# A three-instruction exponential on VectorE with one term made by GpSimd, a shorter rsqrt chain and earlier head preparation in a normalized attention kernel

## The chip, the cores and the metric

The kernel runs on one core of a Trainium2 chip. The metric is device time in microseconds (us). Before the change two runs took 858.82 and 860.21 us, median 859.52. One further execution was profiled; it took 857.78 us, and its span from first to last instruction is 855.5 us.

Names of engines: PE is TensorE (its weight loads are listed as PEld), DVE is VectorE, ACT is ScalarE, POOL is GpSimd, SP is SyncE, whose queue (SPq) issues all DMAs here.

## What is computed

Attention with normalized queries and keys for 32 heads of 2048 positions and 20 channels, in bf16. There is no mask, and no maximum is subtracted, since the logits are bounded by t, which is near 1.

```python
qn = q / (sqrt((q*q).sum(-1)) + eps)
kn = k / (sqrt((k*k).sum(-1)) + eps)
logits = einsum('bhqd,bhkd->bhqk', qn, kn) * t[h]
out = einsum('bhqk,bhkd->bhqd', softmax(logits), v)
```

The costly part is the exponential of 32 x 2048 x 2048 logits.

## The kernel before

**Tiling.** The keys of a head are cut into R = 16 chunks of 128 keys. For one chunk the 2048 queries form four units of 512 (index g). A chunk of logits therefore is a tile of 128 keys by 2048 queries. Most chunks get their exponential on ACT; some get it on DVE. `DVE_TILES` (line 177) says how many chunks of each head go to DVE: 3, 3, 3, 4 and again, so 13 of every 64, 104 of 512 in all. The other 408 chunks are 1632 units for ACT.

**ACT path** (`add_wave`, lines 379 to 404). Three units make a wave: PE writes three products of 128x512 into one half of `psA` (six banks of PSUM, two halves), and ACT takes the exponential of all 1536 columns in one instruction into `p_ring`. There are 544 waves. Where two of the units belong to different halves of the row groups, PE works them side by side with 64 rows each.

**DVE path** (`add_dtile`, lines 417 to 459). It builds the exponential from the bits of an fp16 number. For each of the four units of a chunk, PE writes the logits into `psD`, the only bank for this path, and DVE makes `xt = int16(x * 1024 * log2(e) + offset)`, called t1 here (line 430). Read as fp16, `xt` is a power of two with a linear mantissa. Four further instructions on the whole 128x2048 chunk correct the mantissa: `rr` (an xor, line 435), `mm` (the mantissa as a number in [1, 2), line 437), `tt = xt * mm` (line 440) and `uu = tt * mm` (line 443). PE then adds three products to the output: `xt` with 8 v, `rr` with 2 v, and `uu` with v. The scaled copies `v8` and `v2` are made by POOL once per head (lines 278 to 281).

**Output.** All products of probabilities and values of a head add up in `psO`, one bank. `pv_mm` (line 346) issues four matmuls, one per column group. When a head is complete, DVE transposes `psO` (line 360), takes a reciprocal and scales (`add_fin`), and SP stores the result.

**Preparation of a head** (`add_prep`, line 259). SP loads q, k and v; DVE squares, sums, and makes a reciprocal square root by the integer start value and two Newton steps (lines 290 to 308), in ten small instructions plus the scaling by t; DVE writes the normalized rows `qkn` (line 310). SP then issues a DMA transpose to `qkT` (line 315), four copies to `qz` (line 321) and six rotated copies to `kR` (line 327). The matmuls of the head wait for all of these. `qkT`, `qz` and `kR` have three buffers, so the transpose of head h also waits for the last logits product of head h - 3.

**The order of work.** Every piece is a task with an engine, an assumed duration, dependencies and a due value, in units of heads. `schedule` (line 51) plays the tasks through once with the assumed durations: a free engine takes the ready task with the smallest due value. That gives each engine a fixed order, in which the engine then waits by semaphores. A head's preparation is due at h - 1.6; t1 and the products that feed it have a bonus, so they go ahead of everything else on DVE; the four chunk-wide instructions are due about when ACT reaches that part of the head. `plan_waits` drops waits that others imply.

Of the kernel before, what the change touches and what calls it, by code (L numbers as in the profile page):

```python
# [9 lines left out]
BF16 = mybir.dt.bfloat16  # L10
FP16 = mybir.dt.float16
F32 = mybir.dt.float32
# [4 lines left out]

KEXP = 12.9958  # L20
LOG2E = math.log2(math.e)
X_MUL = 1024.0 * LOG2E
X_ADD = 1024.0 * (15.0 - math.log2(KEXP))


class Task:
# [10 lines left out]
class Program:  # L37
# [8 lines left out]
    def add(self, eng, name, fn, dur, deps=(), pri=0.0, lat=0.0, dma=None):  # L46
        t = Task(eng, name, fn, dur, deps, pri, lat, dma)
        self.tasks.append(t)
        return t
# [54 lines left out]
    def plan_waits(self, sem_of):  # L104
        pos = {}
        for e, ts in self.order.items():
            for i, t in enumerate(ts):
                pos[t.seq] = i
        for t in self.tasks:
            for d in t.deps:  # L110
                if not d.dma and (d.eng != t.eng or d.eng == "DVE"):
                    d.inc = True
        dma_cnt = {}
        for e, ts in self.order.items():
            c = 0
            for t in ts:
                if t.dma:
                    dma_cnt[t.dma] = dma_cnt.get(t.dma, 0) + 16
                    t.cnt = dma_cnt[t.dma]
                elif t.inc:  # L120
                    c += 1
                    t.cnt = c
        allt = sorted(self.tasks, key=lambda t: (t.start, t.seq))
        known = {e: {} for e in self.order}
        snap = {}
        waits = {}
        for t in allt:
            kn = known[t.eng]
            need = {}
            for d in t.deps:  # L130
                if not d.dma and d.eng == t.eng and d.eng != "DVE":
                    continue
                key = d.dma if d.dma else d.eng
                if need.get(key, (0, None))[0] < d.cnt:
                    need[key] = (d.cnt, d)
            ws = []
            for key, (c, d) in sorted(need.items(), key=lambda kv: -kv[1][1].end):
                if kn.get(key, 0) >= c:
                    continue
                ws.append((key, c))  # L140
                kn[key] = c
                for k2, c2 in snap[d.seq].items():
                    if kn.get(k2, 0) < c2:
                        kn[k2] = c2
            waits[t.seq] = ws
            snap[t.seq] = dict(kn)
        self.waits = waits
# [12 lines left out]
def bass_standalone__qk_norm__prompt_kernel(  # L160
# [13 lines left out]
    NB = 4  # L174
    NT = 3
    NX = 3
    DVE_TILES = [4 if h % 4 == 3 else 3 for h in range(H)]
    PE_GROUP = 0.27
    VD = 4

    with ExitStack() as es:
        sbuf = lambda name, shape, dt: es.enter_context(nc.sbuf_tensor(name, shape, dt))
# [3 lines left out]
        act_scr = sbuf("act_scr", [128, 32], F32)  # L186
        qk_sb = [sbuf(f"qk_sb{i}", [128, 2 * R, D], BF16) for i in range(NB)]
        vaug = [sbuf(f"vaug{i}", [128, R, 32], BF16) for i in range(NB)]
        v2 = [sbuf(f"v2{i}", [128, VD, 32], BF16) for i in range(NB)]
        v8 = [sbuf(f"v8{i}", [128, VD, 32], BF16) for i in range(NB)]  # L190
        sq = sbuf("sq", [128, 2 * R, D], F32)
        rs = {x: sbuf(f"rs_{x}", [128, 2 * R], F32) for x in ("sum", "u", "a", "b", "c", "y", "r")}
        qkn = [sbuf(f"qkn{i}", [128, 2 * R, 32], BF16) for i in range(2)]
        qkT = [sbuf(f"qkT{i}", [128, 8 * 128], BF16) for i in range(NT)]
        qz = [sbuf(f"qz{i}", [128, NG, 512], BF16) for i in range(NT)]
        kR = [sbuf(f"kR{i}", [128, 3, 512], BF16) for i in range(NT)]
        p_ring = sbuf("p_ring", [128, NP * 512], BF16)
        xt = [sbuf(f"xt{i}", [128, 2048], I16) for i in range(NX)]
        rr = [sbuf(f"rr{i}", [128, 2048], I16) for i in range(NX)]
        mm = [sbuf(f"mm{i}", [128, 2048], I16) for i in range(2)]  # L200
        tt = [sbuf(f"tt{i}", [128, 2048], FP16) for i in range(2)]
        uu = [sbuf(f"uu{i}", [128, 2048], FP16) for i in range(NX)]
        oT = sbuf("oT", [128, R, 32], F32)
        rec = sbuf("rec", [128, R], F32)
        o_stage = [sbuf(f"o_stage{i}", [128, R * D], BF16) for i in range(2)]
# [40 lines left out]
            return h + (i - a0[h]) / nA_head[h]  # L246


        ld_qk, ld_v, norm, trn, rot, vsc = {}, {}, {}, {}, {}, {}
        qk_users = {h: [] for h in range(H)}  # L250
        pv_users = {h: [] for h in range(H)}
        vs_users = {h: [] for h in range(H)}

        def bc(ap2d, n):
            return bass.AP(ap2d.tensor, ap2d.offset, [ap2d.ap[0], [1, n], [0, D]])
# [2 lines left out]

        def add_prep(h):
            b, b2, bt = h % NB, h % 2, h % NT  # L260
            due = h - 1.6
            war = [norm[h - NB]] if h >= NB else []
            lds = []
            for nh in range(4):
# [6 lines left out]
            lds.append(add("SP", f"ldk{h}", lambda eng, tk: eng.dma_start(qk_sb[b][:, R:2 * R, :], src_k),  # L271
                           0.6, war, due - 0.5, lat=2.5, dma=f"k{b}"))
            src_v = v[0, h].rearrange("(p r) d -> p r d", p=128)
            warv = (pv_users[h - NB] + vs_users[h - NB] + [vsc[h - NB]]) if h >= NB else z_v[b]
            ld_v[h] = add("SP", f"ldv{h}", lambda eng, tk: eng.dma_start(vaug[b][:, :, 0:D], src_v),
                          0.6, warv, due - 0.4, lat=3.0, dma=f"v{b}")

            def vscale(eng, tk):
                eng.tensor_scalar(v2[b][:, :, :], vaug[b][:, R - VD:R, :], 2.0, None, ALU.mult)  # L279
                return eng.tensor_scalar(v8[b][:, :, :], vaug[b][:, R - VD:R, :], 8.0, None, ALU.mult)  # L280
            vsc[h] = add("POOL", f"vsc{h}", vscale, 0.8, [ld_v[h]] + z_v[b], due)

            def dv(name, fn, dur, deps):
                return add("DVE", name + str(h), fn, dur, deps, due)
# [2 lines left out]
                    0.75, lds + prep_deps)]  # L287
            c.append(dv("sum", lambda eng, tk: eng.tensor_reduce(rs["sum"][:, :], sq[:, :, :], AXIS_X, ALU.add),
                        0.75, [c[-1]]))
            c.append(dv("rs", lambda eng, tk: eng.tensor_single_scalar(  # L290
                rs["u"][:, :].bitcast(I32), rs["sum"][:, :].bitcast(I32), 1, ALU.logical_shift_right), 0.12, [c[-1]]))
            c.append(dv("rs", lambda eng, tk: eng.tensor_scalar(
                rs["u"][:, :].bitcast(I32), rs["u"][:, :].bitcast(I32), 1597463007, -1, ALU.subtract, ALU.mult),
                0.12, [c[-1]]))
            cur = rs["u"]
            for it in range(2):
                c.append(dv("rs", lambda eng, tk, cur=cur: eng.tensor_tensor(
                    rs["a"][:, :], cur[:, :], cur[:, :], ALU.mult), 0.12, [c[-1]]))
                c.append(dv("rs", lambda eng, tk: eng.tensor_tensor(
                    rs["b"][:, :], rs["a"][:, :], rs["sum"][:, :], ALU.mult), 0.12, [c[-1]]))  # L300
                c.append(dv("rs", lambda eng, tk: eng.tensor_scalar(
                    rs["c"][:, :], rs["b"][:, :], -0.5, 1.5, ALU.mult, ALU.add), 0.12, [c[-1]]))
                tgt = rs["r"] if it == 1 else rs["y"]
                c.append(dv("rs", lambda eng, tk, cur=cur, tgt=tgt: eng.tensor_tensor(
                    tgt[:, :], cur[:, :], rs["c"][:, :], ALU.mult), 0.12, [c[-1]]))
                cur = rs["y"]
            c.append(dv("rs", lambda eng, tk: eng.tensor_scalar(
                rs["r"][:, 0:R], rs["r"][:, 0:R], t_f32[:, h:h + 1], None, ALU.mult), 0.12, [c[-1], tcp]))
            war = [trn[h - 2]] if h >= 2 else [z_qkn[b2]]
# [69 lines left out]
        def add_wave(w):  # L379
# [13 lines left out]
            deps = [act.get(w - 2)]  # L393
            for h in hs:
                deps += [trn[h]] + rot[h]
            qk = add("PE", f"qkA{w}", f_qk, 0.22 * (len(us) - 1), deps, due_a(us[0]) - 100)
            for h in hs:
                qk_users[h].append(qk)
            p0 = us[0] % NP
# [17 lines left out]
        def add_dtile(j):  # L417
# [7 lines left out]
            for ii in range(NG):  # L425
# [6 lines left out]
                    [qk] + old.get("x", []), due - 5)  # L432
                t1_prev[0] = t1
                t1s.append(t1)
            tr_ = add("DVE", f"r{j}", lambda eng, tk: eng.tensor_single_scalar(  # L435
                rr[s][:, :], xt[s][:, :], 0x3FF, ALU.bitwise_xor), 0.60, t1s + old.get("r", []), due)
            tm = add("DVE", f"m{j}", lambda eng, tk: eng.tensor_scalar(  # L437
                mm[s2][:, :], xt[s][:, :], 0x3FF, 0x3C00, ALU.bitwise_and, ALU.bitwise_or), 0.60,
                t1s + old2.get("m", []), due)
            tT = add("DVE", f"T{j}", lambda eng, tk: eng.tensor_tensor(  # L440
                tt[s2][:, :], xt[s][:, :].bitcast(FP16), mm[s2][:, :].bitcast(FP16), ALU.mult), 1.13,
                [tm] + old2.get("t", []), due)
            tU = add("DVE", f"U{j}", lambda eng, tk: eng.tensor_tensor(  # L443
                uu[s][:, :], tt[s2][:, :], mm[s2][:, :].bitcast(FP16), ALU.mult), 1.13,
                [tT] + old.get("u", []), due)
            b = h % NB
            rv = r - (R - VD)
            base = [vsc[h]] + ([trO[h - 1]] if h else [])

            def pv(nm, tile, wt, deps):  # L450
                p = add("PE", f"pv{nm}{j}", lambda eng, tk: pv_mm(
                    eng, h, wt, lambda g: tile[:, 512 * g:512 * g + 512].bitcast(FP16)), PE_GROUP, deps + base, due + 0.2)
                pv_users[h].append(p)
                return p
            pS = pv("S", xt[s], v8[b][:, rv, :], t1s)
            pR = pv("R", rr[s], v2[b][:, rv, :], [tr_])
            pU = pv("U", uu[s], vaug[b][:, r, :], [tU])
            vs_users[h] += [pS, pR, pU]
            x_users[j] = {"x": [tr_, tm, tT, pS], "r": [pR], "m": [tT, tU], "t": [tU], "u": [pU]}

        d0 = [sum(DVE_TILES[:h]) for h in range(H + 1)]
        nw = ng = 0
# [75 lines left out]
```

## Time and profile before

| | busy, us | share of the span | instructions |
|---|---|---|---|
| PE | 706.3 | 83% | 4836 |
| DVE | 783.2 | 92% | 1380 |
| ACT | 749.7 | 88% | 546 |
| POOL | 52.9 | 6% | 79 |

| | us |
|---|---|
| span of the profiled execution | 855.5 |
| device time of the profiled execution | 857.78 |
| median of two runs | 859.52 |

The time outside the span is thus about 2.3 us, and the profiled execution is 1.7 us under the median. The first matmul starts at 29.4 us and the first exponential of ACT at 30.6 us: until then the first heads are loaded, normalized, transposed and rotated. The mean granted clock of PE is 0.960.

A group of instructions is read as line, engine, operation, what is written and read, count, then busy time and mean duration, then the idle time of the engine just ahead of it and what ended that idle time. Durations in the records of DVE and ACT overlap a little from one instruction to the next, so the sum of the durations on DVE is more than its busy time.

### The profile page before, as it was taken

How to read it: one execution, taken by the hardware profiler on the slowest of the kernel's cores; microseconds unless marked ns; L12 is line 12 of the kernel's file. 1: busy time of each engine (PE TensorE's matmuls, PEld its weight loads, DVE VectorE, ACT ScalarE, POOL GpSimd, SP SyncE). 2: the span in 40 equal slices, each digit the busy share in tenths (PEclk: the TensorE clock that was granted, in tenths of full speed). 3: DMA queues.
4: the chain of work that ended last, by engine and by line, in shares of the span. 5: the costliest groups of instructions: out<-in, count | busy, mean ns of one | idle time of the engine just before them, and what ended most of it. 6: DMA issues, size and time to landing. Idle time of an engine off the chain costs nothing.

```text
span 855.5 us, 12498 instructions
## 1 busy us (share of the span) xinstructions
PE 706.3 (83%) x4836; PEld 201.5 (24%) x4928; DVE 783.2 (92%) x1380; ACT 749.7 (88%) x546; POOL 52.9 (6%) x79
## 2 busy tenths in 40 slices
PE   0598998989887988788986998959988798898887
PEld 0122222222222222122221222212222122222122
DVE  7699998989998999799987999879998899999798
ACT  0599999989999899799986999859998799999797
POOL 3000000001000000000000101000000000000000
PEclk9999999999999999899997999979999899999799
DMA  6441203331213330413314213042121421220200
GB/s 54 89 65 30 49 10 53 53 52 23 47 38 54 53 53 5 67 35 53 47 14 67 54 32 53 8 77 44 31 44 18 80 34 37 45 41 22 66 1 8
DMA packets 198346, 36.49 MB, mean 43 GB/s; under 512 B 173712, under 2 KB 198288, under 8 KB 198288
## 3 DMA queue, kind: packets, MB, share of 16 engines
q1 hardware_dynamic: 198288, 35.70, 25.4%
q8 instruction: 38, 0.62, 0.3%
q14 instruction: 20, 0.16, 0.1%
HBM read 7.87 MB, written 2.62 MB: 12 GB/s over the span
## 4 chain that ended last, share of the span: by engine, by line
DVE 51%; PE 26%; SPq 13%; DMA 4%; issue 3%; ACT 2%
DVE xt L430 19%; PE psA L342 12%; DVE tt L440 9%; PE psO L351 8%; DVE uu L443 8%; PE psD L342 6%; SPq L327 5%; SPq L321 4%; DVE mm L437 3%; SPq L268 3%; DMA kR<-qkT 3%; DVE rr L435 3%; ACT p_ring L402 2%; DVE qkn L310 2%; DVE oT L360 2%
## 5 line engine op out<-in xcount | busy, mean ns | idle before, releaser
L402 ACT ACTIVATE p_ring<-psA 128x1536 bf16<-128x1536 f32 x544 | 748.2, 1463 | 100.4 <-PE psA L342 84.2
L342 PE MATMUL psA<-qz,kR 64*128 64x512 bf16 (+1 forms) x1169 | 316.1, 401 | 61.5 <-DMA kR<-qkT 43.7
L430 DVE TENSOR_SCALAR xt<-psD 128x512 int16<-128x512 f32 x416 | 284.1, 683 | 55.2 <-PE psD L342 50.1
L351 PE MATMUL psO<-p_ring,vaug 128*32 128x512 bf16 x1632 | 165.6, 396 | 8.4 <-issue 5.3
L342 PEld LDWEIGHTS psA<-qz,kR 64*128 64x128 bf16 (+1 forms) x1224 | 85.1, 94 | 267.9 <-issue 163.7
L342 PE MATMUL psD<-qz,kR 128*128 128x512 bf16 x296 | 119.2, 403 | 34.4 <-DVE xt L430 15.7
L342 PE MATMUL psA<-qz,qkT 64*128 64x512 bf16 (+1 forms) x395 | 133.3, 400 | 5.3 <-DMA kR<-qkT 1.8
L443 DVE TENSOR_TENSOR uu<-tt,mm 128x2048 f16<-128x2048 f16 x104 | 126.6, 1217 | 0.0
L440 DVE TENSOR_TENSOR tt<-xt,mm 128x2048 f16<-128x2048 f16 x104 | 126.5, 1216 | 0.1
L435 DVE TENSOR_SCALAR rr<-xt 128x2048 int16<-128x2048 int16 x104 | 71.4, 686 | 0.2
L437 DVE TENSOR_SCALAR mm<-xt 128x2048 int16<-128x2048 int16 x104 | 71.3, 685 | 0.0
L351 PEld LDWEIGHTS psO<-p_ring,vaug 128*32 128x32 bf16 x1632 | 42.0, 93 | 110.7 <-issue 100.9
L279 POOL TENSOR_SCALAR v<-vaug 128x128 bf16<-128x128 bf16 x32 | 21.7, 677 | 701.8 <-DMA vaug<-in_v_dram 701.8
L351 PE MATMUL psO<-uu,vaug 128*32 128x512 f16 x416 | 41.8, 392 | 19.8 <-DVE uu L443 18.7
L342 PEld LDWEIGHTS psD<-qz,kR 128*128 128x128 bf16 x312 | 30.3, 97 | 96.3 <-DVE xt L430 57.7
L342 PEld LDWEIGHTS psA<-qz,qkT 64*128 64x128 bf16 (+1 forms) x408 | 32.6, 94 | 68.6 <-issue 51.7
L351 PE MATMUL psO<-xt,v 128*32 128x512 f16 x416 | 41.4, 388 | 8.1 <-DVE oT L360 5.8
L342 PE MATMUL psD<-qz,qkT 128*128 128x512 bf16 x96 | 38.4, 400 | 6.5 <-DVE xt L430 4.7
L351 PE MATMUL psO<-rr,v 128*32 128x512 f16 x416 | 41.2, 386 | 1.5 <-DVE rr L435 1.1
L286 DVE TENSOR_TENSOR sq<-qk_sb 128x640 f32<-128x640 bf16 x32 | 26.2, 819 | 3.4 <-DMA qk_sb<-in_k_dram 3.2
L280 POOL TENSOR_SCALAR v<-vaug 128x128 bf16<-128x128 bf16 x32 | 27.4, 856 | 2.0
L360 DVE STREAM_TRANSPOSE oT<-psO 128x512 f32<-128x512 f32 x32 | 22.7, 710 | 5.2 <-PE psO L351 4.9
(29 smaller groups left out, 190.9 us busy)
## 6 DMA issues: line engine op xcount, KB each, us to landing
kR<-qkT SPq DMA_DIRECT2D x64, 96.0 KB, 2.1
qz<-qkT SPq DMA_DIRECT2D x128, 32.0 KB, 1.9
kR<-qkT SPq DMA_DIRECT2D x64, 64.0 KB, 2.0
qk_sb<-in_q_dram SPq DMA_DIRECT2D x128, 20.0 KB, 2.5
qk_sb<-in_k_dram SPq DMA_DIRECT2D x32, 80.0 KB, 2.5
vaug<-in_v_dram SPq DMA_DIRECT2D x32, 80.0 KB, 3.2
out_dram<-o_stage SPq DMA_DIRECT2D x32, 80.0 KB, 1.9
kR<-qkT SPq DMA_DIRECT2D x64, 32.0 KB, 1.9
```

The source lines that it names most:

```text
L280: return eng.tensor_scalar(v8[b][:, :, :], vaug[b][:, R - VD:R, :], 8.0, None, ALU.mult)
L321: rot[h].append(add("SP", f"qz{h}", lambda eng, tk, g=g: eng.dma_start(qz[bt][32 * g:32 * g + 32, g, :], qkT[bt][32 * g:32 * g + 32, 0:512 ...
L327: rot[h].append(add("SP", f"rot{h}", lambda eng, tk, d0=d0, s0=s0, m=m, dl=dl: eng.dma_start(kR[bt][d0:d0 + m, dl - 1, :], qkT[bt][s0:s0 + ...
L342: return eng.matmul(dst, lhsT, qz[bt][ps, g, :], tile_position=(p0, 0))
L351: last = eng.matmul(psO[32 * g:32 * g + 32, :], lhsT, rhs_of(g), start=start, stop=False, skip_group_check=True, tile_position=(0, 32 * g))
L360: tr = add("DVE", f"tr{h}", lambda eng, tk: eng.transpose(oT[:, :, :].rearrange("p r d -> p (r d)"), psO[:, :]), 0.62, pv_users[h] + ([fin ...
L402: act[w] = add("ACT", f"exp{w}", lambda eng, tk: eng.activation(p_ring[:, p0 * 512:p0 * 512 + n], psA[:, slot * WAVE * 512:slot * WAVE * 5 ...
L430: t1 = add("DVE", f"t1.{j}.{g}", lambda eng, tk, g=g: eng.tensor_scalar(xt[s][:, 512 * g:512 * g + 512], psD[:, :], X_MUL, X_ADD, ALU.mult ...
L435: tr_ = add("DVE", f"r{j}", lambda eng, tk: eng.tensor_single_scalar(rr[s][:, :], xt[s][:, :], 0x3FF, ALU.bitwise_xor), 0.60, t1s + old.ge ...
L437: tm = add("DVE", f"m{j}", lambda eng, tk: eng.tensor_scalar(mm[s2][:, :], xt[s][:, :], 0x3FF, 0x3C00, ALU.bitwise_and, ALU.bitwise_or), 0.60,
L440: tT = add("DVE", f"T{j}", lambda eng, tk: eng.tensor_tensor(tt[s2][:, :], xt[s][:, :].bitcast(FP16), mm[s2][:, :].bitcast(FP16), ALU.mult ...
L443: tU = add("DVE", f"U{j}", lambda eng, tk: eng.tensor_tensor(uu[s][:, :], tt[s2][:, :], mm[s2][:, :].bitcast(FP16), ALU.mult), 1.13, [tT] ...
```

## The change

The exponential of the DVE path has one product less. The mask of the exponent bits, `ee = (xt & 0x7C00) | 6`, is made by DVE; `ss = xt + (288 - 4096)`, a number with shifted bits, by POOL; `mm` gets another constant; `tt = xt * mm` stays; `uu` and `rr` go. PE adds three products as before, now of `ee`, `ss` and `tt`, all with the same v, so `v2`, `v8` and the POOL instructions that made them go. The rsqrt chain loses its shift and its two separate `c` steps. A head's preparation is due at h - 2.2. The share of chunks on DVE is 3, 4, 4 and again: 117 of 512. Ties in `plan_waits` are ordered by place in the engine's order, and a wave of one unit is assumed to take as long as one of two.

```diff
-    DVE_TILES = [4 if h % 4 == 3 else 3 for h in range(H)]
+    DVE_TILES = [3 if h % 3 == 0 else 4 for h in range(H)]
-    VD = 4
+    SH_ENG, SH_DUR = "POOL", 2.1
...
-            due = h - 1.6
+            due = h - 2.2
...
-            warv = (pv_users[h - NB] + vs_users[h - NB] + [vsc[h - NB]]) if h >= NB else z_v[b]
+            warv = pv_users[h - NB] if h >= NB else z_v[b]
...
-            def vscale(eng, tk):
-                eng.tensor_scalar(v2[b][:, :, :], vaug[b][:, R - VD:R, :], 2.0, None, ALU.mult)
-                return eng.tensor_scalar(v8[b][:, :, :], vaug[b][:, R - VD:R, :], 8.0, None, ALU.mult)
-            vsc[h] = add("POOL", f"vsc{h}", vscale, 0.8, [ld_v[h]] + z_v[b], due)
...
-            c.append(dv("rs", lambda eng, tk: eng.tensor_single_scalar(
-                rs["u"][:, :].bitcast(I32), rs["sum"][:, :].bitcast(I32), 1, ALU.logical_shift_right), 0.12, [c[-1]]))
             c.append(dv("rs", lambda eng, tk: eng.tensor_scalar(
-                rs["u"][:, :].bitcast(I32), rs["u"][:, :].bitcast(I32), 1597463007, -1, ALU.subtract, ALU.mult),
+                rs["u"][:, :].bitcast(I32), rs["sum"][:, :].bitcast(I32), -0.5, 1597463007.0, ALU.mult, ALU.add),
                 0.12, [c[-1]]))
             cur = rs["u"]
-            for it in range(2):
+            for tgt in (rs["y"], rs["r"]):
                 c.append(dv("rs", lambda eng, tk, cur=cur: eng.tensor_tensor(
                     rs["a"][:, :], cur[:, :], cur[:, :], ALU.mult), 0.12, [c[-1]]))
...
+                c.append(dv("rs", lambda eng, tk: eng.scalar_tensor_tensor(
+                    rs["b"][:, :], rs["a"][:, :], -0.5, rs["sum"][:, :], ALU.mult, ALU.mult), 0.12, [c[-1]]))
+                c.append(dv("rs", lambda eng, tk, cur=cur, tgt=tgt: eng.scalar_tensor_tensor(
+                    tgt[:, :], rs["b"][:, :], 1.5, cur[:, :], ALU.add, ALU.mult), 0.12, [c[-1]]))
...
-            tr_ = add("DVE", f"r{j}", lambda eng, tk: eng.tensor_single_scalar(
-                rr[s][:, :], xt[s][:, :], 0x3FF, ALU.bitwise_xor), 0.60, t1s + old.get("r", []), due)
+            te = add("DVE", f"e{j}", lambda eng, tk: eng.tensor_scalar(
+                ee[s][:, :], xt[s][:, :], 0x7C00, KE_BITS, ALU.bitwise_and, ALU.bitwise_or), 0.60,
+                t1s + old.get("e", []), due)
+            t5 = add(SH_ENG, f"s{j}", lambda eng, tk: eng.tensor_scalar(
+                ss[s][:, :], xt[s][:, :], float(SHIFT - 4096), None, ALU.add), SH_DUR, t1s + old.get("s", []), due)
             tm = add("DVE", f"m{j}", lambda eng, tk: eng.tensor_scalar(
-                mm[s2][:, :], xt[s][:, :], 0x3FF, 0x3C00, ALU.bitwise_and, ALU.bitwise_or), 0.60,
+                mm[s2][:, :], xt[s][:, :], 0x3FF, 0x3800, ALU.bitwise_and, ALU.bitwise_or), 0.60,
                 t1s + old2.get("m", []), due)
             tT = add("DVE", f"T{j}", lambda eng, tk: eng.tensor_tensor(
-                tt[s2][:, :], xt[s][:, :].bitcast(FP16), mm[s2][:, :].bitcast(FP16), ALU.mult), 1.13,
-                [tm] + old2.get("t", []), due)
-            tU = add("DVE", f"U{j}", lambda eng, tk: eng.tensor_tensor(
-                uu[s][:, :], tt[s2][:, :], mm[s2][:, :].bitcast(FP16), ALU.mult), 1.13,
-                [tT] + old.get("u", []), due)
+                tt[s][:, :], xt[s][:, :].bitcast(FP16), mm[s2][:, :].bitcast(FP16), ALU.mult), 1.13,
+                [tm] + old.get("t", []), due)
...
-            pS = pv("S", xt[s], v8[b][:, rv, :], t1s)
-            pR = pv("R", rr[s], v2[b][:, rv, :], [tr_])
-            pU = pv("U", uu[s], vaug[b][:, r, :], [tU])
+            pE, pS, pT = pv("E", ee[s], te), pv("S", ss[s], t5), pv("T", tt[s], tT)
+            x_users[j] = {"x": [te, t5, tm, tT], "e": [pE], "s": [pS], "m": [tT], "t": [pT]}
```

More of the change, by code (lines that the diff above doesn't have):

```diff
@@ L16 @@
 AXIS_X = mybir.AxisListType.X
-KEXP = 12.9958
+KEXP = 0.63116
+KE_BITS = 6
+SHIFT = 288
 LOG2E = math.log2(math.e)
 X_MUL = 1024.0 * LOG2E
-X_ADD = 1024.0 * (15.0 - math.log2(KEXP))
+X_ADD = 1024.0 * (15.0 + math.log2(KEXP))
 class Task:
@@ L122, in plan_waits @@
                     t.cnt = c
-        allt = sorted(self.tasks, key=lambda t: (t.start, t.seq))
+        allt = sorted(self.tasks, key=lambda t: (t.start, pos[t.seq]))
         known = {e: {} for e in self.order}
@@ L188, in bass_standalone__qk_norm__prompt_kernel @@
         vaug = [sbuf(f"vaug{i}", [128, R, 32], BF16) for i in range(NB)]
-        v2 = [sbuf(f"v2{i}", [128, VD, 32], BF16) for i in range(NB)]
-        v8 = [sbuf(f"v8{i}", [128, VD, 32], BF16) for i in range(NB)]
         sq = sbuf("sq", [128, 2 * R, D], F32)
-        rs = {x: sbuf(f"rs_{x}", [128, 2 * R], F32) for x in ("sum", "u", "a", "b", "c", "y", "r")}
+        rs = {x: sbuf(f"rs_{x}", [128, 2 * R], F32) for x in ("sum", "u", "a", "b", "y", "r")}
         qkn = [sbuf(f"qkn{i}", [128, 2 * R, 32], BF16) for i in range(2)]
@@ L198, in bass_standalone__qk_norm__prompt_kernel @@
         xt = [sbuf(f"xt{i}", [128, 2048], I16) for i in range(NX)]
-        rr = [sbuf(f"rr{i}", [128, 2048], I16) for i in range(NX)]
+        ee = [sbuf(f"ee{i}", [128, 2048], I16) for i in range(NX)]
+        ss = [sbuf(f"ss{i}", [128, 2048], I16) for i in range(NX)]
         mm = [sbuf(f"mm{i}", [128, 2048], I16) for i in range(2)]
-        tt = [sbuf(f"tt{i}", [128, 2048], FP16) for i in range(2)]
-        uu = [sbuf(f"uu{i}", [128, 2048], FP16) for i in range(NX)]
+        tt = [sbuf(f"tt{i}", [128, 2048], FP16) for i in range(NX)]
         oT = sbuf("oT", [128, R, 32], F32)
@@ L246, in due_a @@
             return h + (i - a0[h]) / nA_head[h]
-        ld_qk, ld_v, norm, trn, rot, vsc = {}, {}, {}, {}, {}, {}
+        ld_v, norm, trn, rot = {}, {}, {}, {}
         qk_users = {h: [] for h in range(H)}
         pv_users = {h: [] for h in range(H)}
-        vs_users = {h: [] for h in range(H)}
         def bc(ap2d, n):
@@ L289, in add_prep @@
                         0.75, [c[-1]]))
-            c.append(dv("rs", lambda eng, tk: eng.tensor_single_scalar(
-                rs["u"][:, :].bitcast(I32), rs["sum"][:, :].bitcast(I32), 1, ALU.logical_shift_right), 0.12, [c[-1]]))
             c.append(dv("rs", lambda eng, tk: eng.tensor_scalar(
-                rs["u"][:, :].bitcast(I32), rs["u"][:, :].bitcast(I32), 1597463007, -1, ALU.subtract, ALU.mult),
+                rs["u"][:, :].bitcast(I32), rs["sum"][:, :].bitcast(I32), -0.5, 1597463007.0, ALU.mult, ALU.add),
                 0.12, [c[-1]]))
             cur = rs["u"]
-            for it in range(2):
+            for tgt in (rs["y"], rs["r"]):
                 c.append(dv("rs", lambda eng, tk, cur=cur: eng.tensor_tensor(
                     rs["a"][:, :], cur[:, :], cur[:, :], ALU.mult), 0.12, [c[-1]]))
[L299 to L306, printed above, removed]
+                c.append(dv("rs", lambda eng, tk: eng.scalar_tensor_tensor(
+                    rs["b"][:, :], rs["a"][:, :], -0.5, rs["sum"][:, :], ALU.mult, ALU.mult), 0.12, [c[-1]]))
+                c.append(dv("rs", lambda eng, tk, cur=cur, tgt=tgt: eng.scalar_tensor_tensor(
+                    tgt[:, :], rs["b"][:, :], 1.5, cur[:, :], ALU.add, ALU.mult), 0.12, [c[-1]]))
+                cur = tgt
             c.append(dv("rs", lambda eng, tk: eng.tensor_scalar(
@@ L395, in add_wave @@
                 deps += [trn[h]] + rot[h]
-            qk = add("PE", f"qkA{w}", f_qk, 0.22 * (len(us) - 1), deps, due_a(us[0]) - 100)
+            qk = add("PE", f"qkA{w}", f_qk, 0.22 * max(1, len(us) - 1), deps, due_a(us[0]) - 100)
             for h in hs:
@@ L443, in add_dtile @@
-            tU = add("DVE", f"U{j}", lambda eng, tk: eng.tensor_tensor(
-                uu[s][:, :], tt[s2][:, :], mm[s2][:, :].bitcast(FP16), ALU.mult), 1.13,
-                [tT] + old.get("u", []), due)
[L446 to L450, printed above, removed]
+                tt[s][:, :], xt[s][:, :].bitcast(FP16), mm[s2][:, :].bitcast(FP16), ALU.mult), 1.13,
+                [tm] + old.get("t", []), due)
@@ L451, in pv @@
+            wt = vaug[h % NB][:, r, :]
+            base = [ld_v[h]] + z_v[h % NB] + ([trO[h - 1]] if h else [])
+            def pv(nm, tile, dep):
                 p = add("PE", f"pv{nm}{j}", lambda eng, tk: pv_mm(
-                    eng, h, wt, lambda g: tile[:, 512 * g:512 * g + 512].bitcast(FP16)), PE_GROUP, deps + base, due + 0.2)
+                    eng, h, wt, lambda g: tile[:, 512 * g:512 * g + 512].bitcast(FP16)), PE_GROUP, [dep] + base,
+                    due + 0.2)
                 pv_users[h].append(p)
@@ L454, in pv @@
                 return p
-            pS = pv("S", xt[s], v8[b][:, rv, :], t1s)
-            pR = pv("R", rr[s], v2[b][:, rv, :], [tr_])
-            pU = pv("U", uu[s], vaug[b][:, r, :], [tU])
-            vs_users[h] += [pS, pR, pU]
-            x_users[j] = {"x": [tr_, tm, tT, pS], "r": [pR], "m": [tT, tU], "t": [tU], "u": [pU]}
+            pE, pS, pT = pv("E", ee[s], te), pv("S", ss[s], t5), pv("T", tt[s], tT)
+            x_users[j] = {"x": [te, t5, tm, tT], "e": [pE], "s": [pS], "m": [tT], "t": [pT]}
```

## Prediction

> **What bounds the kernel now.** I read the page's busy shares and chain first, then the groups by line, then the waits, then the timeline.
>
> ```profile
> PE 706.3 (83%) x4836; PEld 201.5 (24%) x4928; DVE 783.2 (92%) x1380; ACT 749.7 (88%) x546; POOL 52.9 (6%) x79
> ...
> DVE 51%; PE 26%; SPq 13%; DMA 4%; issue 3%; ACT 2%
> ...
> L402 ACT ACTIVATE p_ring<-psA 128x1536 bf16<-128x1536 f32 x544 | 748.2, 1463 | 100.4 <-PE psA L342 84.2
> L430 DVE TENSOR_SCALAR xt<-psD 128x512 int16<-128x512 f32 x416 | 284.1, 683 | 55.2 <-PE psD L342 50.1
> L443 DVE TENSOR_TENSOR uu<-tt,mm 128x2048 f16<-128x2048 f16 x104 | 126.6, 1217 | 0.0
> L440 DVE TENSOR_TENSOR tt<-xt,mm 128x2048 f16<-128x2048 f16 x104 | 126.5, 1216 | 0.1
> L435 DVE TENSOR_SCALAR rr<-xt 128x2048 int16<-128x2048 int16 x104 | 71.4, 686 | 0.2
> L437 DVE TENSOR_SCALAR mm<-xt 128x2048 int16<-128x2048 int16 x104 | 71.3, 685 | 0.0
> ```
>
> DVE leads: 92% busy and half of the chain. But ACT (88%) and PE (83%) are close behind, so relief of DVE alone is soon capped. SPq 13% and DMA 4% of the chain are the second bound: head preparation that lands late. The chain in order of time (start, us, what), with ACT's own record of that moment from the timeline:
>
> ```profile
> 559.53 0.64 SPq L268
> ...
> 567.27 2.13 DMA kR<-qkT
> ...
> 570.63 2.79 ACT L402 ACTIVATE p_ring<-psA 128x1536 bf16<-128x1536 f32 x2 [8.22 <-PE psA L342]
> ```
>
> The chain runs through the DMA issues, then the landing of `kR`; ACT stands for 8.22 us meanwhile. ACT's idle stretches over 1 us after the first two waves add up to about 46 us; DVE has 21 waits over 0.8 us after the start, 36 us in all, nearly all at the same places.
>
> The third view is POOL beside DVE, at the two small POOL instructions that scale v:
>
> ```profile
> 164.34 1.22 DVE L440 TENSOR_TENSOR tt<-xt,mm 128x2048 f16<-128x2048 f16 x1
> 164.41 1.53 POOL L279 TENSOR_SCALAR v<-vaug 128x128 bf16<-128x128 bf16 x1 [30.04 <-DMA vaug<-in_v_dram]
> 165.48 0.68 DVE L430 TENSOR_SCALAR xt<-psD 128x512 int16<-128x512 f32 x1
> 166.01 0.53 POOL L280 TENSOR_SCALAR v<-vaug 128x128 bf16<-128x128 bf16 x1
> 166.08 1.30 DVE L443 TENSOR_TENSOR uu<-tt,mm 128x2048 f16<-128x2048 f16 x1
> ```
>
> A POOL instruction of 0.53 us takes 1.53 when it meets `tt`, and ends 0.38 us after it. The other way round, `uu`, behind a POOL instruction, takes 1.30 instead of 1.22. t1 keeps its 0.68.
>
> [...] So `ee`, `mm` and `tt` all contend with POOL; t1, which reads PSUM, does not.
>
> **The change part by part.** From one instruction's start to the next, t1 takes 0.60 us, `rr` and `mm` 0.61, `tt` and `uu` 1.13 (timeline; records overlap by some 0.08).
>
> - *DVE per chunk.* Before: 4 x 0.60 + 2 x 0.61 + 2 x 1.13 = 5.88. After: t1 four times, `ee` (same form as the `mm` row, 0.61), `mm`, `tt`: 4.75. Chunks: 104 x 5.88 = 612 to 117 x 4.75 = 556, **-56 us**.
> - *rsqrt chain.* Three instructions fewer per head (one shift, two `c`), at about 0.13 start to start: 96 x 0.13 = **-12 us**. The fused steps have no row; nearest is the 128x32 tensor_tensor, 187 ns; from 0 to 0.05 more each, 128 of them, 0 to +6; I take 0. DVE's busy time becomes 783 - 68 = 715.
> - *ACT.* 1580 units, 527 waves, at 748.2 / 544 = 1.375 each: 724, **-24 us**.
> - *PE.* Steps are 0.32 us apart where the tile shape changes, 0.22 where not. 17 waves less of two steps (-10.9), 13 groups less (-4.2), 39 groups more of the DVE path and 52 more `psD` products at 0.27 (+24.6): +9 us on 706, beside ACT and DVE. I cost it at nothing; DVE's work covers it, thinly: 715 against 715.
> - *The alternation.* `psD` is one bank, so after t1 the next waits for PE: about 0.65 us from the end of one record to the next start with work between (t1 starts at 230.08 and 231.41). Before, four chunk-wide instructions filled four such gaps; now three do. The fourth gap, 117 x 0.65 = 76 us, is filled by head work (about 4.7 us start to start per head, against 3.7 gaps of 0.65) where the fixed order puts it there: 0 to 76, I take 10.
> - *Preparation at h - 2.2.* It moves each head's eleven DVE instructions and, behind them on SP's queue, the transpose, four `qz` and six `kR` issues, and five loads and `v`. From `qkn` to the landing of `kR` took some 13 us (233 to 246) and ended just too late; 0.6 heads is some 15 us (825 / 32 x 0.6). So most of the long waits should go: 30 of DVE's 36, 40 of ACT's 46. What is late next is the ring of three: the transpose of h waits for the last product of h - 3, at h - 2, and stores and `v` loads queue behind it on SP. That leaves two heads, 50 us, against 13, and two output buffers; cost nothing.
> - *v2, v8.* 64 POOL instructions go, and DVE's stretching by them, which I counted from the timeline: 24 of 64 met a contending DVE instruction, 2.3 us in all. Wave tie and planner length: nothing, they only alter the order of equals.
> - *ss on POOL, the unknown.* No row has 2048 elements. The memsets show 0.83 ns per element (418 ns for 384, 1804 for 2048); so streaming holds the ports about 1.7 us, an estimate[...]. It becomes ready together with `ee`. `ee` starts first, [...]t1 (0.60) passes, then `mm` stands: 1.7 - 0.6 = **1.1 us per chunk** at most in that order. At least: 0, if POOL yields between portions. Below nothing only the 2.3 us above. A middle: the small instructions held the ports 64 x 0.107 = 6.8 us and DVE lost 2.3, a third; a third of 1.7 is 0.57. I take **0.3**, between 0 and that third, since with one chunk-wide instruction less, DVE has more t1 and empty gaps under which POOL can stream: 117 x 0.3 = **+35 us**.
> - *The added wait on PE.* The product of `ss` stands in PE's fixed order as if POOL needed 2.1 us; with `ee` ahead it needs nearer 3. Behind it stand the next `psA` wave and `psD` unit; ACT has a second half of `psA`, 1.37 us of cover. 0 to 117 x 0.7 = 82; I take 0, with the upper end in the range.
>
> The sum, for the profiled execution. DVE's idle before was 72: 14 at start and end, 58 after, of which 30 go. 715 + 14 + 28 + 10 + 35 = 802. ACT alone: 724 + 31 ahead of the first wave + 5 behind the last + (72 - 40) = 792. They are 10 apart and the orders are fixed, so I add 6: span 808. With 2.3 outside the span and 1.7 by which the median exceeds the profiled execution: **812 us**.
>
> **The rivals.**
> 1. *POOL holds the ports whole.* 1.1 us per chunk: 767 + 129 = 896, **900 us**. For it: each DVE delay in the trace, about 0.09, is near the 0.107 that 128 elements stream. Against: no row here shows a long POOL instruction, and a part may fall under empty gaps. It decides above 0.9 us per chunk (767 + 105 + 4 = 876). Should POOL need twice the time, over 1000.
> 2. *A part of the hold shows*, 0.6 to 0.9 us per chunk, or PE's wait for `ss` costs as much: 842 to 876.
> 3. *Preparation stays late*, SP's queue blocked by the ring of three: the 30 us stay, 842. Against: 50 us of room.
> 4. *POOL costs nothing*: ACT bounds, 792 + 4 = 796; below that only if its short waits vanish as well, 784.
>
> **How the numbers follow.** This measurement can tell about 2% from no change, 842 to 877. The forecast with rival 4 (below 842): 0.65, of which the forecast alone, 800 to 842, has 0.48 and rival 4 0.17. Rivals 2 and 3: 0.15. Rival 1: 0.20. The range leaves out the upper half of rival 1 and 0.05 below: 784 to 890.
>
> **What would show it.** Right: groups `ee`, `mm`, `tt` at 0.69, 0.69 and 1.22 with hardly any stretch or idle ahead of them; DVE and ACT both over 90%; ACT's stretches over 2 us gone. Wrong: `mm` or `tt` with a mean 0.5 or more above, or gaps behind t1 while POOL streams; POOL means above 3 us; PE idle put down to POOL `ss`; transposes on SP waiting for PE.

## The result

The changed kernel takes 1416.3 us (median of 2 runs) against 859.52 before: a ratio of 1.648, 95% interval 1.640 to 1.656. It is far slower, where the prediction had 812 us, in a range of 784 to 890. The profiled execution took 1417.34 us, its span is 1415.5.

The first lines of the page after, and the groups that answer to those shown of before:

```profile
PE 941.5 (67%) x5032; PEld 211.4 (15%) x5032; DVE 1219.4 (86%) x1271; ACT 748.6 (53%) x529; POOL 680.1 (48%) x132
...
DVE 53%; PE 38%; POOL 3%; issue 3%; SPq 1%; ACT 1%; POOLq 0%; DMA 0%; ACTq 0%; DVEq 0%
...
L392 ACT ACTIVATE p_ring<-psA 128x1536 bf16<-128x1536 f32 x527 | 747.1, 1451 | 662.1 <-PE psA L332 659.7
L428 POOL TENSOR_SCALAR ss<-xt 128x2048 int16<-128x2048 int16 x117 | 676.3, 5780 | 719.4 <-DVE xt L420 625.7
L420 DVE TENSOR_SCALAR xt<-psD 128x512 int16<-128x512 f32 x468 | 319.4, 682 | 159.6 <-PE psD L332 156.9
...
L430 DVE TENSOR_SCALAR mm<-xt 128x2048 int16<-128x2048 int16 x117 | 385.2, 3292 | 0.0
L425 DVE TENSOR_SCALAR ee<-xt 128x2048 int16<-128x2048 int16 x117 | 251.0, 2145 | 0.6
...
L433 DVE TENSOR_TENSOR tt<-xt,mm 128x2048 f16<-128x2048 f16 x117 | 141.4, 1209 | 0.2
```

Read the means. `mm` had 685 ns before and has 3292; `ee` is the same form and has 2145. Neither has idle time ahead of it: the instruction counts as busy while it stands and waits (5.25 us for the `mm` below). That is why DVE still shows 86% and why a share of busy time would mislead here. One `ss` on POOL takes 5.78 us, not the 2.1 that was planned. ACT is idle for 662 us ahead of its waves; it starves.

One chunk of the changed kernel in the timeline (start, duration, engine):

```profile
221.55 0.69 DVE L425 TENSOR_SCALAR ee<-xt 128x2048 int16<-128x2048 int16 x1
...
221.59 5.88 POOL L428 TENSOR_SCALAR ss<-xt 128x2048 int16<-128x2048 int16 x1 [8.22 <-DVE xt L420]
...
222.16 0.68 DVE L420 TENSOR_SCALAR xt<-psD 128x512 int16<-128x512 f32 x1
...
222.76 5.25 DVE L430 TENSOR_SCALAR mm<-xt 128x2048 int16<-128x2048 int16 x1
...
227.52 0.11 PEld L341 LDWEIGHTS psO<-ss,vaug 128*32 128x32 bf16 x4 [3.38 <-POOL ss L428]
227.52 0.62 PE L341 MATMUL psO<-ss,vaug 128*32 128x512 f16 x4 [3.08 <-POOL ss L428]
```

`ee` starts first and runs undisturbed; `ss` begins behind it; t1 passes in 0.68; `mm` stands until POOL ends at 227.47 and finishes half a microsecond later. In every one of the 117 chunks one of the two stands like this, `mm` in 76 and `ee` in the other 41, and it ends 0.54 to 0.55 us after POOL's `ss`. This is rival 1 of the prediction, at another price. PE waits too: its product of `ss` stands in front of everything else. When it goes on, a matmul takes 0.62 us (0.53 on average for this product), where the products into `psO` took about 0.39 before; the mean granted clock is 0.775 against 0.960.

So there is one theory with three rivals. **Theory P**: `ee` and `mm` stand while POOL's long instruction runs, and all else follows. (The recorded texts speak of ports and of a port theory. That it is ports was assumed; no run here shows what holds `ee` and `mm` up.) **Rivals**: A, the new fixed orders, with the alternation on `psD`; B, SP's queue blocked by the earlier preparation; C, PE's wait for `ss`.

### The profile page after: what moved, and what is told of

It is laid out like the page before. It is cut to its first block, busy times and chain, and to the rows that moved or that the text cites. A ratio compares the mean times of both kernels' runs of the same rounds, so it can differ in the third digit from the quotient of the medians.

```text
span 1415.5 us, 12746 instructions
## 1 busy us (share of the span) xinstructions
PE 941.5 (67%) x5032; PEld 211.4 (15%) x5032; DVE 1219.4 (86%) x1271; ACT 748.6 (53%) x529; POOL 680.1 (48%) x132
## 4 chain that ended last, share of the span: by engine, by line
DVE 53%; PE 38%; POOL 3%; issue 3%; SPq 1%; ACT 1%; POOLq 0%; DMA 0%; ACTq 0%; DVEq 0%
DVE mm L430 22%; PE psA L332 16%; DVE ee L425 14%; PE psO L341 13%; DVE xt L420 10%; PE psD L332 9%; POOL ss L428 3%; DVE tt L433 2%; DVE o_stage L355 1%; DVE oT L350 1%; ACT p_ring L392 1%; SPq L268 1%; DVE sq L281 1%; DVE rs_sum L283 0%; POOLq L184 0%
## 5 line engine op out<-in xcount | busy, mean ns | idle before, releaser
L428 POOL TENSOR_SCALAR ss<-xt 128x2048 int16<-128x2048 int16 x117 | 676.3, 5780 | 719.4 <-DVE xt L420 625.7
L420 DVE TENSOR_SCALAR xt<-psD 128x512 int16<-128x512 f32 x468 | 319.4, 682 | 159.6 <-PE psD L332 156.9
L332 PE MATMUL psA<-qz,kR 64*128 64x512 bf16 (+1 forms) x1185 | 397.1, 485 | 30.2 <-DMA kR<-qkT 28.2
L430 DVE TENSOR_SCALAR mm<-xt 128x2048 int16<-128x2048 int16 x117 | 385.2, 3292 | 0.0
L425 DVE TENSOR_SCALAR ee<-xt 128x2048 int16<-128x2048 int16 x117 | 251.0, 2145 | 0.6
L332 PE MATMUL psD<-qz,kR 128*128 128x512 bf16 x351 | 175.0, 499 | 103.4 <-DVE xt L420 101.1
L332 PE MATMUL psA<-qz,qkT 64*128 64x512 bf16 (+1 forms) x395 | 163.7, 487 | 1.3 <-ACT p_ring L392 1.0
L341 PE MATMUL psO<-ss,vaug 128*32 128x512 f16 x468 | 62.6, 525 | 91.2 <-POOL ss L428 91.1
L341 PE MATMUL psO<-ee,vaug 128*32 128x512 f16 x468 | 57.0, 477 | 96.6 <-DVE ee L425 91.6
L341 PE MATMUL psO<-tt,vaug 128*32 128x512 f16 x468 | 61.2, 515 | 6.7 <-DVE tt L433 6.6
```

The lines of the kernel that those rows point to most:

```text
L332: return eng.matmul(dst, lhsT, qz[bt][ps, g, :], tile_position=(p0, 0))
L341: last = eng.matmul(psO[32 * g:32 * g + 32, :], lhsT, rhs_of(g), start=start, stop=False, skip_group_check=True, tile_position=(0, 32 * g))
L420: t1 = add("DVE", f"t1.{j}.{g}", lambda eng, tk, g=g: eng.tensor_scalar(xt[s][:, 512 * g:512 * g + 512], psD[:, :], X_MUL, X_ADD, ALU.mult ...
L425: te = add("DVE", f"e{j}", lambda eng, tk: eng.tensor_scalar(ee[s][:, :], xt[s][:, :], 0x7C00, KE_BITS, ALU.bitwise_and, ALU.bitwise_or), ...
L428: t5 = add(SH_ENG, f"s{j}", lambda eng, tk: eng.tensor_scalar(ss[s][:, :], xt[s][:, :], float(SHIFT - 4096), None, ALU.add), SH_DUR, t1s + ...
L430: tm = add("DVE", f"m{j}", lambda eng, tk: eng.tensor_scalar(mm[s2][:, :], xt[s][:, :], 0x3FF, 0x3800, ALU.bitwise_and, ALU.bitwise_or), 0.60,
```

## The experiments

### The changed kernel without ss, and with POOL work that nobody waits for

```diff
-            t5 = add(SH_ENG, f"s{j}", ... ss[s] ... SH_DUR, ...)
-            pE, pS, pT = pv("E", ee[s], te), pv("S", ss[s], t5), pv("T", tt[s], tT)
+            pE, pS, pT = pv("E", ee[s], te), pv("S", ee[s], te), pv("T", tt[s], tT)
```

> The changed kernel without the POOL instruction: the product that used ss takes ee instead, so the shifted term is left out of the result; DVE, ACT and SP are asked for the same otherwise. Port theory[...]: all of the loss goes, ee and mm back at 0.69 us each, the time about 785 to 815 us, and TensorE's granted clock back above 0.9. Rival A (the three balanced engines in their new fixed orders, and the psD alternation with one chunk-wide instruction less, make the loss): above 900 us. Rival B (the earlier preparation blocks SP's queue): stretches of ACT over 2 us remain.

Then the same with scratch work on POOL, started when `ss` was. No engine waits for it; PE, DVE and ACT have the same instructions in the same order as in the kernel without `ss`.

```diff
+            dum[j] = add("POOL", f"d{j}", lambda eng, tk: eng.tensor_scalar(
+                dy[s][:, :], dx[:, :], float(SHIFT - 4096), None, ALU.add), 5.4, t1s + ..., due)
```

> As noss, with a POOL tensor_scalar of 128x2048 int16 per chunk on scratch tiles, started as ss was; nobody waits for its result (the shifted term stays left out). Port theory: most of the loss is back without any wait of TensorE for POOL; ee or mm stretched by about 4 us per chunk, 1250 to 1400 us. Rival C (TensorE's wait for ss in its fixed order makes the loss): within 3% of noss.

Measured: without `ss` 781.33 us, a ratio of 0.911 to before (0.908 to 0.914), a little under the 785 to 815 expected. With the scratch work 1436.98 us in one run, somewhat above the 1250 to 1400 expected. From the page of the kernel without `ss`, then the groups of the one with scratch work:

```profile
PE 714.6 (92%) x5032; PEld 201.9 (26%) x5032; DVE 720.3 (92%) x1271; ACT 725.5 (93%) x529; POOL 3.8 (0%) x15
...
L425 DVE TENSOR_SCALAR ee<-xt 128x2048 int16<-128x2048 int16 x117 | 80.1, 685 | 0.7
L428 DVE TENSOR_SCALAR mm<-xt 128x2048 int16<-128x2048 int16 x117 | 79.9, 683 | 0.0
```

```profile
L432 POOL TENSOR_SCALAR dy<-dx 128x2048 int16<-128x2048 int16 x117 | 674.4, 5764 | 741.4 <-DVE xt L424 653.8 <-DVE rs_u L288 87.6
L434 DVE TENSOR_SCALAR mm<-xt 128x2048 int16<-128x2048 int16 x117 | 399.7, 3416 | 0.0
...
L429 DVE TENSOR_SCALAR ee<-xt 128x2048 int16<-128x2048 int16 x117 | 260.2, 2224 | 0.7
```

Theory P holds, and C falls: work on other data, for which nobody waits, costs as much as `ss` did. A and B fall too. Without POOL, the balanced engines and the early preparation give 92, 92 and 93% busy, and only one wait of ACT above 2 us is left (3.35 us, at 52 us). The planner orders PE and DVE somewhat differently there than in the changed kernel, so the pair with one and the same order, 781 and 1437, is the stronger evidence against A. What the runs show is that POOL's work holds up `ee` and `mm`: means of 685 and 683 ns without it, 2224 and 3416 beside it. By what, was not shown.

Where the loss lies: from the kernel without `ss` to the changed one the span grows by 1415.5 - 780.7 = 635 us. DVE's busy time grows by 499; of that, `ee` and `mm` have 385.2 + 251.0 - 2 x 80 = 476, and the scaling of the output, which stands behind POOL in six places, has 14. DVE's idle time grows from 60 to 196, by 136. That part lies mostly ahead of t1, waiting for PE (157 us against 27.5), and PE has waits and a lower granted clock then (0.775 against 0.993); which of the two makes how much was not separated.

### Is it reading or writing, and how long does a short piece hold?

The scratch work as a memset, and as 16 instructions of 128 columns. (In the first expectation, "writes and reads nothing" means that a memset only writes.)

```diff
+            dum[j] = add("POOL", f"d{j}", lambda eng, tk: eng.memset(dy[s][:, :], 0), 1.8, ...)
```

> As noss_d2048, but the scratch work is a memset of 128x2048 16-bit elements, which writes and reads nothing (1.8 us in the kernel before). Port theory[...]: ee or mm[...] stand about 1.2 us per chunk[...]; 880 to 960 us. If only POOL's reading excludes DVE: as noss.

```diff
+                for c in range(16):
+                    last = eng.tensor_scalar(dy[s][:, 128 * c:128 * c + 128], dx[:, 128 * c:128 * c + 128], ...)
```

> As noss_d2048, but the scratch work of a chunk is cut into 16 POOL instructions of 128 columns. If POOL holds the ports for its whole instruction: the same total hold or more, as slow as noss_d2048 or slower. If a short instruction holds them only while it reads (the delays of about 0.09 us that the small scalings of v caused in the kernel before): about 16 x 0.1 = 1.6 us of DVE per chunk or less, 850 to 1000 us, and POOL 16 x 0.53 = 8.5 us per chunk, 117 x 8.5 = 994 us of POOL work, which then sets the end at about 1030.

Measured: 953.12 us for the memset. Its groups:

```profile
L429 DVE TENSOR_SCALAR ee<-xt 128x2048 int16<-128x2048 int16 x117 | 237.3, 2028 | 0.7
L432 POOL MEMSET dy<- 128x2048 int16 x117 | 211.3, 1806 | 721.3 <-DVE xt L424 721.3
L436 DVE TENSOR_TENSOR tt<-xt,mm 128x2048 f16<-128x2048 f16 x117 | 141.5, 1209 | 0.1
L433 DVE TENSOR_SCALAR mm<-xt 128x2048 int16<-128x2048 int16 x117 | 79.1, 676 | 0.0
```

A memset that only writes stops `ee` as well, by 1.7 us at the most (2.38 is its longest). So POOL work that reads nothing is enough. `tt` is never stretched (1.23 us at the most), but no `tt` starts while a memset runs here, so this run says nothing of it. The direct stretch, 157 us, gives most of the 172 between this and the run without POOL work.

The 16 pieces: 1353.04 us, not the 1030 or so expected, but this end is POOL's own: it needs 1196.5 us for its pieces where 994 were expected. It works through its backlog alone; the last store of the result is issued at 793 us, against 779 us without POOL work. The groups:

```profile
L434 POOL TENSOR_SCALAR dy<-dx 128x128 int16<-128x128 int16 x1872 | 1196.5, 639 | 148.5 <-DVE xt L424 29.4
...
L438 DVE TENSOR_SCALAR mm<-xt 128x2048 int16<-128x2048 int16 x117 | 88.7, 758 | 0.0
L429 DVE TENSOR_SCALAR ee<-xt 128x2048 int16<-128x2048 int16 x117 | 83.4, 713 | 0.7
```

POOL is busy nearly without a break up to that store, and yet `ee` and `mm` are at 0.71 and 0.76 us. The hold is not the time that POOL instructions run.

### ss itself, in pieces

The full result again, with `ss` cut along the columns. The diff is that for 512; the others differ in width and in the planned duration.

```diff
-    SH_ENG, SH_DUR = "POOL", 2.1
+    SH_ENG, SH_DUR = "POOL", 6.2
...
+                for c in range(0, 2048, 512):
+                    last = eng.tensor_scalar(ss[s][:, c:c + 512], xt[s][:, c:c + 512], ...)
```

> The changed kernel with ss cut into four POOL instructions of 512 columns, planned at 6.2 us. If the hold grows with the length of one instruction faster than in proportion[...] (16 pieces of 128 cost DVE only some 22 us of busy time in all): clearly faster than the changed kernel, 900 to 1250 us. If DVE's mean ee and mm together stay above 5 us: the whole instruction is held at 512 as at 2048, and only the gaps between the pieces are gained, 1300 to 1420 us.

> The same with eight instructions of 256 columns, planned at 7.2 us. POOL has 8 x 0.85 = 6.8 us of work per chunk (line through 0.53 us for 128 columns and 5.37 for 2048), 117 x 6.8 = 796 us, with its waits for DVE some 850 to 950, which then sets the end if DVE is let through as with 128 columns; if 256 columns are held whole, above 1200 us.

> The changed kernel with ss cut into two POOL instructions of 1024 columns. In pieces of 128, 256 and 512 columns DVE's instructions were stretched by at most about 0.1, 0.2 and 0.41 us: the columns of a piece at 0.83 ns each[...]. [...]stretches of at most 0.85 us, ee and mm means below 1.3 us, the time 870 to 960 us. [...]stretches reach 1.5 to 2.6 us: 1050 to 1400 us.

(For 1024, the first forecast has stretches of 0.83 ns per column, the second of up to the 2.5 ns per column that `ss` itself takes, 5.37 us for 2048 columns against 0.53 for 128.)

Measured in one run each: 897.11 us (512), 1078.73 (256), 876.86 (1024). The instructions `ee` by piece, minimum, median and maximum in ns, first for 1024, then 512, then 256:

```profile
L425 DVE TENSOR_SCALAR ee<-xt x117: 642/739/1548, 35.8 to 864.1; 128x2048 int16<-128x2048 int16 x117
```

```profile
L425 DVE TENSOR_SCALAR ee<-xt x117: 629/695/1139, 35.3 to 883.0; 128x2048 int16<-128x2048 int16 x117
```

```profile
L425 DVE TENSOR_SCALAR ee<-xt x117: 679/722/926, 36.2 to 1055.1; 128x2048 int16<-128x2048 int16 x117
```

Over the usual 0.69, the worst stretches are 0.86, 0.45 and 0.24 us: close to 1024, 512 and 256 columns at the 0.83 ns of POOL's memsets (418 ns for 384 columns, 1804 for 2048). For the whole 2048 it was 5.2 us instead of 1.7. The piece of 1024 itself lasts at least 2.77 us, so up to there DVE does not stand for a whole piece. For 256 the expectation of 850 to 950 was missed: POOL, at a mean of 1.04 us for a piece, becomes the bound with 976 us of work, and PE and t1 wait for it. At 512 too POOL is the busiest engine (92%). At 1024 DVE leads again with 94%. The times for 1024 and 512 lie at the low end of what was expected, 512 just below it. None of the cuts beats the kernel before, which took 856 to 857 us beside them.

### ss on DVE, and the share of chunks

```diff
-    SH_ENG, SH_DUR = "POOL", 2.1
+    SH_ENG, SH_DUR = "DVE", 0.6
```

> The changed kernel with ss made by DVE (0.69 us recorded, 0.61 start to start) and nothing on POOL in the loop. Port theory: DVE's work becomes that of noss plus 117 x 0.61 = 71 us, and DVE bounds: span about 781 + 50 to 75, that is 830 to 855 us. If POOL beside DVE were not the matter: above 1000 us.

With 13 of 64 chunks, and with 107 of 512:

```diff
-    DVE_TILES = [3 if h % 3 == 0 else 4 for h in range(H)]
+    DVE_TILES = [4 if h % 4 == 3 else 3 for h in range(H)]
```

> As ss_dve, with 13 of 64 chunks on DVE as before the change: DVE work 13 x (4.75 + 0.61) = 70 us less, ACT 17 waves more (23 us). ACT then bounds: 748 + 36 around + 20 of waits, 800 to 820 us, faster than both kernels.

```diff
-    DVE_TILES = [3 if h % 3 == 0 else 4 for h in range(H)]
+    DVE_TILES = [4 if h % 3 == 1 else 3 for h in range(H)]
```

> As ss_dve_13 with 107 chunks on DVE instead of 104: ACT 4 waves less, 5.5 us; DVE 3 x 5.36 = 16 us more, 732 against ACT's 742. If ACT alone bounds, about 5 us under ss_dve_13 (799 us); if the two wait for each other, the same within 3 us.

| chunks on DVE, ss on DVE | median, us | ratio to before (95%) | DVE busy | ACT busy |
|---|---|---|---|---|
| 117 | 822.79 | 0.961 (0.959 to 0.964) | 779.9 | 727.1 |
| 107 | 798.68 | 0.932 (0.929 to 0.935) | 724.3 | 741.9 |
| 104 | 804.43 | 0.939 (0.935 to 0.942) | 716.1 | 746.4 |

All three beat both kernels. Moving one instruction of 0.69 us from POOL to DVE takes the changed kernel from 1416 to 823 us, a little under the 830 to 855 expected. With `ss` there, 117 chunks are too many, since DVE leads ACT by 53 us. 107 has the lowest time, but its 0.7% over 104 is no clear difference: the two were not measured together, and the intervals of their ratios touch.

### The other parts alone, on the kernel before

```diff
-            due = h - 1.6
+            due = h - 2.2
```

> The kernel before with the preparation due at h - 2.2 and nothing else. As predicted: DVE's and ACT's long waits at the change of heads go, 30 of 58 us of DVE's idle: 825 to 840 us. If SP's queue blocks on the ring of three: no gain, 850 to 865 us.

The rsqrt chain as in the change, on the kernel before:

> The kernel before with the shorter rsqrt chain and nothing else. As predicted, 96 instructions of 0.13 us less on DVE: 12 us less if DVE bounds everywhere, 842 to 852 us; if the waits at the change of heads take it up, 850 to 860.

Measured: 815.51 us for the preparation (ratio 0.952, 0.949 to 0.955), 830.07 for the chain (0.969, 0.966 to 0.972). The ACT group of the first:

```profile
L402 ACT ACTIVATE p_ring<-psA 128x1536 bf16<-128x1536 f32 x544 | 745.3, 1474 | 57.0 <-PE psA L342 54.3 <-PE psO L351 0.4
```

ACT's idle time falls from 100.4 to 57.0 us. Its waits over 1 us after the start fall from 17 with 48 us to 6 with 7.6. SP's queue did not block. Both parts alone gave more than expected (825 to 840, and 842 to 852). The chain brought more than DVE's own saving: DVE's busy time fell by 783.2 - 768.4 = 15 us, the time by 27 against the runs beside it, and ACT's long waits from 48 to 26 us.

## Why the prediction was wrong

**The step that failed** is the term "ss on POOL, the unknown": 0.3 us per chunk, 35 us in all, with 1.1 as the most. Measured directly on `ee` and `mm` it is (2145 + 3292 - 2 x 685) / 1000 = 4.07 us per chunk, 476 us; with the waits that follow, 635. Two things were wrong in it, its price above all.

- *The price of the instruction.* I took the memsets' 0.83 ns per column for `ss` as well, an estimate. No run with a POOL `TENSOR_SCALAR` agrees: `ss` took 5.37 us at the least for 2048 columns, and with 0.53 for 128 that is 2.5 ns per column, three times as much. With 5.37 in place of 1.7, the prediction's own order gives 5.37 - 0.6 = 4.8 us per chunk, not far from the 4.07 measured. The trace of before had the nearer row, a POOL `TENSOR_SCALAR` of 128 columns. Less 0.1 us, what a memset of one column takes (101 ns), its 0.53 allows up to 3.4 ns per column, or 6.9 us for 2048. This upper bound was not worked out, and the range rested on the lower one.
- *The third.* I scaled DVE's loss from the short instructions, and took about half of that. The short ones were no measure of the long one: a piece of 128 delays by 0.1 us, one of 2048 by 5.2, fifty times as much for sixteen times the columns.

What was **right**: `ee` and `mm` contend with POOL and t1 does not. In the trace of after `mm` takes 3.29 us on average, and no t1 more than 0.70, with 94 of the 468 starting while `ss` runs. For the form of `ee` and `mm` the trace of before has it on a small scale: three `rr` and one `mm` took 0.76 to 0.79 us instead of 0.69, each of them beside a POOL instruction. `tt` took up to 1.89 us instead of 1.21 beside pieces of 1024. That `ee` goes first and `mm` stands was right for 76 of the 117 chunks. That POOL holds for its whole instruction fits the 2048 columns (5.2 of 5.4 us), and not the pieces (0.86 of 2.77 us for 1024). Rival 1 decided; its price was put at 1.1 instead of 4.1, and it was given a chance of 0.20. That POOL might need more time was said there (twice the time, over 1000 us), but the range left it out.

**The rest of the sum held.** The kernel without `ss` tests it. DVE's busy time: 715 predicted, 720.3 measured. ACT: 724 and 725.5. PE: 706 + 9 and 714.6, which is in part luck, since the trace of before lacks 92 of 4928 matmul records and its clock is lower (0.960 against 0.993). "POOL costs nothing": 796 predicted, 781 measured, below even the 784 that the prediction gave as its lowest; ACT is idle for 55 us there, where the sum had 31 + 5 + 32 = 68. The chain alone was put at 12 us and brought 27; why so much was not found out. Rival 3 was wrong: of ACT's ten waits over 2 us, one stayed.

The wait of PE for `ss`, costed at nothing, is there (91 us ahead of its matmuls), but adds nothing to the loss that could be seen: without it the time was 1437.

## What to carry to other kernels

An instruction moved to an idle engine is not free if it holds up the busy one, as here (781 us without POOL's work, 1437 with it on data for which nobody waits): price the time for which the other stands, and take that price from a row of the same operation on the same engine, with the upper bound that its fixed part allows. A mean far above the shortest of its group, without idle time ahead of it, can be a wait in disguise (`mm`: 3.29 us against 0.62). And test such a move by running the work on scratch data: if the loss stays while nobody waits for the result, it is the work of the two side by side and not the dependency.

## What was unexpected of the hardware

How long POOL holds DVE up does not follow the duration of its instruction. Pieces of 128, 256, 512 and 1024 columns stretched `ee` by at most 0.12, 0.24, 0.45 and 0.86 us, while the pieces lasted 0.53, 0.85, 1.49 and 2.77 us or more; one of 2048 columns held for 5.2 of its 5.4 us.

The trace with pieces of 1024 shows where in a piece the hold lies. Two pieces, each with the instructions of DVE that start while it runs:

```profile
352.62 2.77 POOL L430 TENSOR_SCALAR ss<-xt 128x1024 int16<-128x1024 int16 x1 [0.96 <-DVE xt L420]
353.82 0.65 DVE L420 TENSOR_SCALAR xt<-psD 128x512 int16<-128x512 f32 x1
354.40 1.54 DVE L425 TENSOR_SCALAR ee<-xt 128x2048 int16<-128x2048 int16 x1
...
361.28 3.27 POOL L430 TENSOR_SCALAR ss<-xt 128x1024 int16<-128x1024 int16 x1 [2.73 <-DVE xt L420]
361.84 1.52 DVE L434 TENSOR_SCALAR mm<-xt 128x2048 int16<-128x2048 int16 x1
363.29 0.68 DVE L420 TENSOR_SCALAR xt<-psD 128x512 int16<-128x512 f32 x1
363.89 1.21 DVE L437 TENSOR_TENSOR tt<-xt,mm 128x2048 f16<-128x2048 f16 x1
```

`ee`, 1.0 us before the end of its piece, stands 0.85 us; `mm`, 0.56 us after the start of its piece, stands about as long; `tt`, 0.66 us before the end, does not stand. The whole trace agrees. Of the 56 `ee`, `mm` and `tt` that start in the first 0.8 us of a piece, 49 stand, by at most 0.84 us. All 60 `ee` and `mm` that start in its last 0.2 to 1.0 us stand, until some 0.14 us before its end, but none of the 79 `tt` that start there. In between (from 1.3 us on), 36 of 38 are not delayed. In the changed kernel the output's scaling, a product of two tensors like `tt`, is let go well before `ss` ends (its own end is 1.39 us ahead of that of `ss` each of six times), `ee` and `mm` only at the end.

So a piece of 1024 holds DVE up at both of its ends, each time by no more than about its columns at the 0.83 ns of a memset (0.85 us), and hardly in between; `tt` stands only at the first end. At 2048 columns no such middle is seen: all 117 `ee` and `mm` that start between 0.23 and 5.0 us after `ss` stand until it ends. No run shows why, and pieces between 1024 and 2048 were not tried.
